# Attention, max-MoE and SoLU-MoE in one kernel: the h blocks of the first two token pairs loaded by two thirds, in other places, with no load held for them

## The chip, the cores and the metric

The kernel runs on one core of one Trainium2 chip. The metric is device microseconds of one execution. Before the change the median of 3 runs is 658.96 us (658.83 to 658.99).

## The reference, cut to what matters

```python
def _attn_ref(q, k, v):                      # 4 batches, 12 heads, 448 tokens, head 64
    scores = matmul(q, k.T) / sqrt(64) - log(448)
    attn = 1 / (1 + exp(-scores))
    return matmul(attn, v)

def _moe_ref(x, w1, w2, w3, w_out):          # x: 1792 tokens x 768
    h = maximum(maximum(x @ w1, x @ w2), x @ w3)
    return h @ w_out

def _moe2_ref(x, w_in, w_out, g_ln):         # w_in: 768 x 1024, w_out: 1024 x 768
    h = x @ w_in
    sm = softmax(h)                          # exp(h - max) / (sum + 1e-9)
    solu = h * sm
    ln = (solu - mean(solu)) / sqrt(var(solu) + 1e-6) * g_ln
    return ln @ w_out

out = _moe2_ref(_moe_ref(_attn_ref(q, k, v), ...), ...)
```

All arrays are float32.

## The kernel before, in words

Every float32 operand of a large product is split in two parts, hi and lo, and the product is three matmuls (hi hi, hi lo, lo hi). A split is a cast on ScalarE (L51) for hi and a subtraction on VectorE (L56) for lo. The large products use a recursion of seven products in place of eight (P1 to P7, table `PROD`): their operands are sums of quarter blocks, named A11, A12, A22, S1 to S4 on one side and B11, B21, B22, T1 to T4 on the other.

The stages:

- Attention for 24 pairs of heads. Beside it `w_out` of the first MoE and `w_in` of the second are multiplied into one matrix, whose seven operands go to DRAM (`w_d`, seven pieces of 128x3x1024 words, 1536 KB each, called B11 to T4 in the list `LOADS`).
- The products of x with w1, w2, w3, in 18 units: nine groups of weights (`gi`) by two batch pairs (`bp`). The last group takes batch pair 1 first, then batch pair 0. `sums` takes the maximum over the three weights in the tiles `hs` and stores every finished third of h (`fp`) to DRAM, `h_d` (L675, L679). The raw words of the weights come through five buffers `raw` (`RAWS`), issued by GpSimd (L141).
- The L stage: h times the fused matrix, in 7 pairs of token tiles. For each pair the four blocks `a` of h are loaded from `h_d` by SP (`load_h`, L710), `prep_l` makes the seven operands from them, and then come P1 (B11), P2 (B21), P6 (T2), P5 (T1), P7 (T3), and behind the next pair's P1 still P4 (T4) and P3 (B22), nine matmuls each. TensorE's timeline names them XL, ZL, XL, VL, XL, XL, VL. The seven weights `wf` are loaded once, by GpSimd (`load_wf`, L739), in the order of `LOADS`.
- Between the two lies `solu_ln`, the normalisation: exponential, squares, a few steps of two columns (`st`), a pair of activations `h`, a transposition on VectorE, a store and a load. Its steps wait in the queue `lazy`.
- The O stage: the second product, again 7 pairs, twelve matmuls a product.

Where the weights of the L stage land is memory that the unit before still uses, so their places come free one after the other: `sa` (tags 0, 1) after the seventh product of the last unit of batch pair 1, `sb` (2, 3, 4) two products later in the next unit, `sc` (5, 6) when the last unit of all is done (L1180 to L1184).

Before the change the first pair's blocks lie in the pool `afirst`. They are loaded by two thirds (the third third of h is not yet in DRAM) and the last third is copied by VectorE out of `hs` (`last_rows`). Between the load of B11 and that of B21 GpSimd makes two small copies of these blocks into a tile `gate` (`hold`, L735), so that B21 is issued only when they have landed:

```python
load_wf(LOADS[0], 0)
load_h(0, 0, slice(0, 2))
load_h(0, 1, slice(0, 2))
for k in range(2):
    hold(hts[(0, 1, k)][:, :8])
last_rows(0)
load_wf(LOADS[1], 1)
```

The order of work on TensorE, ScalarE and VectorE is the order in which the program is written. GpSimd's is pinned from the last units on (`loads`); SP's is set by the scheduler. Work for the next product is interleaved by generators: `run_bg` in the x stage, at a rate per matmul (`RATE`), and `pace(dt)` in the L and O stages: each matmul gives a credit of `dt` microseconds, and steps of `bg`, and then of `lazy`, are taken while credit is left, each with a cost. `product_c` has `dt` 0.227 for the L stage and 0.174 for the O stage.

Of the kernel before, what the change touches and what calls it, by code (L numbers as in the profile page):

```python
# [6 lines left out]
F32 = mybir.dt.float32  # L7
# [8 lines left out]
P = 128  # L16
B, H, S, D = 4, 12, 448, 64
# [11 lines left out]
HU = 384  # L29
QU, OU = 192, 96  # L30
NG = 3 * FC // 2
RAWS = 5
# [12 lines left out]
def sigmoid_attention_max_moe_solu_ln(tc, q, k, v, w123, wo, wi, w2, g, out):  # L45
# [3 lines left out]
    def copy(eng, dst, src):  # L49
        if eng is act:  # L50
            act.copy(dst, src)  # L51
        else:
            eng.tensor_copy(dst, src)
# [68 lines left out]
    raws = {}  # L122
# [199 lines left out]
    def run_bg(n=1):  # L322
        while n > 0 and bg:
            if next(bg[0], "end") == "end":
                bg.popleft()
            else:
                n -= 1
# [324 lines left out]
    def sums(u, i, j, ps, add):  # L652

        gi, bp = u
        fp, w = divmod(gi, 3)
        b = 2 * bp + j
        if (i, b) not in hs:
            nm, n = FIN[len(hs)]
            while (1, nm, n) in fts:
                run_bg()  # L660
            hs[(i, b)] = f_tile(nm, n, f"hs{i}_{b}")
        h = hs[(i, b)]
        if w == 0:
            if add is None:
                act.copy(h, ps)
            else:
                tt(h, ps, add, ALU.add)
        elif add is None:
            tt(h, ps, h, ALU.max)
        else:  # L670
            tt(add, ps, add, ALU.add)
            tt(h, add, h, ALU.max)
        if w == 2:
            to, c = h_d[i, bp][:, :, fp], j * D
            sp.dma_start(  # L675
                out=to[4 * j : 4 * j + 3].rearrange("t p c -> p t c"),
                in_=h[:, c : c + 3 * P].rearrange("p (t c) -> p t c", t=3),
            )
            sp.dma_start(out=to[3, :, c : c + D], in_=h[:, 3 * P * (1 - j) :][:, :D])  # L679
# [16 lines left out]
    hts = {}  # L696

    def h_tile(p, i, k):
        if p % 2:
            t = f_tile(*FIN[4 + i + 2 * k], f"a{p}_{i}{k}")[:, :HU]  # L700
        else:
            t = afirst.tile([P, HU], F32, tag=f"a{i}{k}", name=f"a{p}_{i}{k}")
        hts[(p, i, k)] = t
        return t.rearrange("p (f t) -> p f t", f=3)

    def load_h(p, k, rows=slice(0, 3)):

        for i in range(2):
            bp, t = divmod(tiles[2 * p + i], TT // 2)
            sp.dma_start(out=h_tile(p, i, k)[:, rows], in_=h_d[k, bp][t][:, rows])  # L710

    def last_rows(k):

        for i in range(2):
            t = tiles[i]
            b, c0 = divmod(t * P, S)
            copy(dve, hts[(0, i, k)][:, 2 * P :], hs[(k, b)][:, c0 : c0 + P])

    units = [(gi, bp if gi < NG - 1 else 1 - bp) for gi in range(NG) for bp in range(2)]
    bg.extend(split_t(1, nm, i) for nm, i in FIN)  # L720
# [12 lines left out]
    def hold(view):  # L733

        pool.tensor_copy(gate, view)  # L735

    def load_wf(nm, tag):
        t = wfs[("L", nm)] = wslot[tag].tile([P, 3, 2, 512], F32R, tag=f"s{tag}", name=f"wf{nm}")
        pool.dma_start(out=t.bitcast(F32).rearrange("p c a b -> p c (a b)"), in_=w_d[nm][:, :, : 2 * 512])  # L739
# [125 lines left out]
    for n, u in enumerate(units):  # L865
        if n % 2 == 0:
            late = run_steps(convert_w2(key) for key in w2_left[n // 2])
            lead = 14 if len(w2_left[n // 2]) > 1 else 4
            bg.append(mix(late, convert_group(u[0] + 1), lead) if u[0] + 1 < NG else late)
        tick.update(n=0, done=0, rate=RATE[n // 2])  # L870
        X = ps_x.tile([P, 512], F32, tag="x", name=f"x{n}")[:, :S]
        product(X, u, "P1", True, False)
        e1 = held(u, "e1", X)
        if old is not None:
            product(old["X"], old["u"], "P4", False, True)
            sums(old["u"], 1, 0, old["X"], None)
            product(old["V"], old["u"], "P3", False, True)
            sums(old["u"], 0, 1, old["V"], old["u2"])
            if old["u"] == (NG - 1, 1):
                run_bg(1 << 20)  # L880
                shut(xc_cm, xb_cm)
                wslot.update(weight_slots("sb", (2, 3, 4)))
                hf_cm, hfirst = open_pool("hfirst", 2)
                last_rows(1)
                for k in range(2):
                    load_h(1, k)
                for tag in (2, 3, 4):
                    load_wf(LOADS[tag], tag)
        Z = ps_z.tile([P, 512], F32, tag="z", name=f"z{n}")[:, :S]
        product(Z, u, "P2", True, True)  # L890
        sums(u, 0, 0, Z, e1)
        product(X, u, "P6", False, False)
        u2 = held(u, "u2", X)
        if n == len(units) - 1:
            bg.append(prep_l(0))
        V = ps_v.tile([P, 512], F32, tag="v", name=f"v{n}")[:, :S]
        product(V, u, "P5", True, False)
        product(X, u, "P7", False, False)
        u3 = held(u, "u3", X)
        sums(u, 1, 1, V, u3)  # L900
        if u == (NG - 1, 1):
            loads = pin(ET.Pool)
            shut(xd_cm)
            wslot.update(weight_slots("sa", (0, 1)))
            af_cm, afirst = open_pool("afirst", 1)
            load_wf(LOADS[0], 0)
            load_h(0, 0, slice(0, 2))
            load_h(0, 1, slice(0, 2))
            for k in range(2):
                hold(hts[(0, 1, k)][:, :8])  # L910
            last_rows(0)
            load_wf(LOADS[1], 1)
        old = dict(u=u, X=X, V=V, u2=u2)
    assert not raws and state["load"] == len(stream)

# [24 lines left out]
    def product_c(ps, kind, p, name, start, stop):  # L940
        a, bn = PROD[name]
        key = (kind, p, a)
        while key not in cops:
            assert step(bg), key
        hl = cops.pop(key)
        wt = wfs[(kind, bn)]
        chunks, dt = (3, 0.227) if kind == "L" else (4, 0.174)
        for c in range(chunks):
            for i, (l, m) in enumerate(((0, 0), (0, 1), (1, 0))):
                pe.matmul(  # L950
                    ps,
                    lhsT=hl[l][:, c * P : (c + 1) * P],
                    rhs=wt[:, c, m],
                    start=(start and c == 0 and i == 0),
                    stop=(stop and c == chunks - 1 and i == 2),
                    skip_group_check=True,
                )
                if c == chunks - 1 and i == 2:
                    spent.add(key)
                pace(dt)  # L960
# [208 lines left out]
    for n, (kind, g) in enumerate(groups):  # L1169
        p, last = g[-1], n == len(groups) - 1  # L1170
        if prev and len(prev) > 1:
            for o in prev:
                fourth(o)
        now_open = [begin(kind, g[0])]
        if n == 0:
            product(old["X"], old["u"], "P4", False, True)
            sums(old["u"], 1, 0, old["X"], None)
            product(old["V"], old["u"], "P3", False, True)
            sums(old["u"], 0, 1, old["V"], old["u2"])
            for cm in (xat_cm, xau_cm, xa_cm, st_cm, raw_cm):  # L1180
                shut(cm)
            wslot.update(weight_slots("sc", (5, 6, 7), side="right"))
            for tag in (5, 6):
                load_wf(LOADS[tag], tag)  # L1184
            t_cm, tp = open_pool("tp", 2, side="right")
            act.preload_act_table_set("natural_log_exp_and_others")
        else:
            close(prev)
        now_open += [begin(kind, p) for p in g[1:]]
        if n == 2:  # L1190
            load_w2(LOADS[0], 7)
        if (kind, p) == ("L", NP2 - 1):
            load_u(1)
        if not last:
            for o in now_open:
                second(o)
        if (kind, p) == ("O", 1):
            load_u(2)
        for o in now_open:
            sixth(o)  # L1200
        if kind == "L":
            if p + 2 < NP2:
                next_h(p + 2)
            if p == NP2 - 2:
                load_u(0)
            bg.append(prep_l(p + 1) if p + 1 < NP2 else in_turn(prep_o(0), prep_o(1), 1))
        elif not last:
            bg.append(prep_o(p + 1))
            if 1 < p < NP2 - 2:
                load_u(p + 2)  # L1210
        for o in now_open:
            fifth(o)
        for o in now_open:
            seventh(o)
        if (kind, p) == ("O", 1):
            load_u(3)
        if last:
            for o in now_open:
                second(o)
        prev = now_open  # L1220
# [61 lines left out]
```

## Time and profile before

| | |
|---|---|
| median of 3 runs | 658.96 us |
| profiled execution | 658.38 us |
| its span | 656.6 us |
| TensorE busy | 637.8 us (97%) |
| VectorE busy | 490.7 us (75%) |
| ScalarE busy | 373.4 us (57%) |
| GpSimd busy | 72.6 us (11%) |
| granted clock, mean | 0.992 |

The span runs from the first to the last event on the core; the execution's time is 1.8 us longer. A timeline row gives the start, the length, the engine, the line, what is written from what, how many instructions are merged, and in brackets how long the engine stood idle before, with what ended it. SPq and POOLq are the queues in which SP and GpSimd issue DMAs. A windows row gives busy time by engine in one stretch, then the granted clock of TensorE (PEclk, 1.00 is full speed), the mean busy share of the core's 16 DMA engines, and what they moved. Releasers are inferred: where the engine named had long been done, it was another.

### The profile page before, as it was taken

The page shows a single profiled execution, that of the slowest core. Times are in us where ns is not written, and L with a number is a line of the kernel's source. Part 1 is how long each engine was busy: PE and PEld are TensorE (multiplying, and loading weights), DVE is VectorE, ACT ScalarE, POOL GpSimd, SP SyncE. Part 2 cuts the span into 40 slices and gives each one's busy share as a digit, 9 for nine tenths or more (in the row PEclk, how much of TensorE's full clock was granted, in tenths as well). Part 3 has the DMA queues.
Part 4 walks back from the last instruction along what each step waited for, and adds up shares of the span by engine and source line. Part 5 has one row for each costly group of instructions (what it writes and reads, how often), then busy time and mean ns, then how long its engine had stood idle before and what let it go on. Part 6 is the DMA issues. An engine that isn't in the chain of part 4 may idle for free.

```text
span 656.6 us, 9719 instructions
## 1 busy us (share of the span) xinstructions
PE 637.8 (97%) x3283; PEld 519.3 (79%) x3283; DVE 490.7 (75%) x1070; ACT 373.4 (57%) x712; POOL 72.6 (11%) x147
## 2 busy tenths in 40 slices
PE   9999999999999999999999999977999999999897
PEld 6555588754557999999999999955877889999897
DVE  4799987599547788886888678544688879687672
ACT  5888523578866545455455454222666674766551
POOL 2111121000100101101101100112000035300000
PEclk9999999999999999999999999997999999999999
DMA  8688668853710346765468543899336269956151
GB/s 292 216 256 260 220 199 303 314 211 109 259 33 0 105 125 188 215 166 163 131 176 233 168 121 90 248 374 407 130 108 182 58 205 385 311 180 185 59 168 70
DMA packets 85921, 125.17 MB, mean 191 GB/s; under 512 B 39024, under 2 KB 65648, under 8 KB 85872
## 3 DMA queue, kind: packets, MB, share of 16 engines
q1 hardware_dynamic: 74288, 70.84, 34.2%
q0 software_dynamic: 11440, 53.48, 25.2%
q8 instruction: 26, 0.43, 0.3%
q10 hardware_dynamic: 144, 0.23, 0.1%
q14 instruction: 23, 0.19, 0.1%
HBM read 84.15 MB, written 40.37 MB: 190 GB/s over the span
## 4 chain that ended last, share of the span: by engine, by line
PE 65%; DVE 16%; ACT 6%; DMA 6%; issue 5%; SPq 1%; POOL 0%; DVEq 0%; ACTq 0%; POOLq 0%
PE x L644 19%; PE v L644 9%; PE XO L950 7%; PE av L272 6%; PE z L644 5%; PE XL L950 5%; PE sc L251 4%; PE VO L950 4%; PE VL L950 2%; PE ZO L950 2%; DMA wfT<-w_dT 2%; ACT e L998 2%; PE sc L247 1%; DMA wfB<-w_dB 1%; ACT h L1014 1%
## 5 line engine op out<-in xcount | busy, mean ns | idle before, releaser
L272 PE MATMUL av<-sf,vr 128*64 128x448 f32 x384 | 77.5, 545 | 0.0
L259 ACT ACTIVATE sf<-sc,bias_s 128x896 f32<-128x896 f32 x72 | 67.9, 1013 | 2.4
L141 POOL DMA_DIRECT2D raw<-in_w x52 | 28.0, 539 | 277.3 <-DVE S L56 138.4
L272 PEld LDWEIGHTS av<-sf,vr 128*64 128x64 f32 x384 | 25.4, 136 | 40.9 <-issue 34.4
L251 PE MATMUL sc<-qt,kt 64*128 64x448 f32 x432 | 51.1, 375 | 1.5 <-ACT sf L256 1.5
L473 PE MATMUL pw<-wi_t,r_wo 128*128 128x512 f32 x216 | 49.6, 390 | 0.0
L251 PEld LDWEIGHTS sc<-qt,kt 64*128 64x128 f32 x432 | 39.0, 184 | 11.7 <-issue 4.3
L473 PEld LDWEIGHTS pw<-wi_t,r_wo 128*128 128x128 f32 x216 | 40.4, 188 | 9.4 <-issue 1.0
L689 ACT COPY u<-x 128x448 f32<-128x448 f32 x36 | 19.1, 530 | 44.3 <-PE x L644 44.3
L950 PE MATMUL XL<-wfT,c_L_S 128*128 128x512 f32 x126 | 33.1, 409 | 4.1 <-DMA wfT<-w_dT 3.1
L644 PE MATMUL x<-T3h,S 128*128 128x448 f32 x108 | 33.7, 366 | 0.0
L644 PE MATMUL x<-B11h,A 128*128 128x448 f32 x108 | 33.7, 366 | 0.0
L644 PE MATMUL x<-T4h,A 128*128 128x448 f32 x108 | 33.6, 365 | 0.0
L644 PE MATMUL x<-T2h,S 128*128 128x448 f32 x108 | 33.6, 365 | 0.0
L644 PE MATMUL v<-B22h,S 128*128 128x448 f32 x108 | 33.6, 365 | 0.0
L644 PE MATMUL z<-B21h,A 128*128 128x448 f32 x108 | 33.6, 365 | 0.0
L644 PE MATMUL v<-T1h,S 128*128 128x448 f32 x108 | 33.6, 365 | 0.0
L950 PEld LDWEIGHTS XL<-wfT,c_L_S 128*128 128x128 f32 x126 | 24.3, 196 | 11.3 <-issue 4.2
L413 ACT ACTIVATE raw<-raw,g_sb 128x192 f32<-128x192 f32 x32 | 13.3, 466 | 31.3 <-DVE raw L157 31.3
L950 PE MATMUL XO<-w2tT,c_O_S 128*128 128x384 f32 x168 | 31.1, 336 | 0.0
L157 DVE SCALAR_TENSOR_TENSOR raw<-raw 128x384 int32<-128x384 int32 x52 | 29.0, 557 | 1.1
L950 PEld LDWEIGHTS XO<-w2tT,c_O_S 128*128 128x128 f32 x168 | 29.3, 188 | 0.0
(185 smaller groups left out, 1547.1 us busy)
## 6 DMA issues: line engine op xcount, KB each, us to landing
raw<-in_w POOLq DMA_DIRECT2D x52, 384.0 KB, 4.1
w_d<-w2s SPq DMA_DIRECT2D x48, 192.0 KB, 2.4
u_d<-h SPq DMA_DIRECT2D x56, 128.0 KB, 2.9
ut<-u_d SPq DMA_DIRECT2D x14, 512.0 KB, 5.3
kr<-in_k SPq DMA_DIRECT2D x24, 256.0 KB, 3.5
vr<-in_v SPq DMA_DIRECT2D x24, 256.0 KB, 3.9
raw<-in_wi POOLq DMA_DIRECT2D x16, 384.0 KB, 4.9
w_dT<-wsT SPq DMA_DIRECT2D x12, 512.0 KB, 3.7
```

What stands on the lines that cost most here:

```text
L141: pool.dma_start(out=t, in_=source(key).rearrange("p (n t) -> p n t", t=2))
L157: dve.scalar_tensor_tensor(out=yi, in0=raws[key][:, cols, 0], scalar=29, in1=yi, op0=ALU.logical_shift_right, op1=ALU.bitwise_or)
L247: pe.matmul(sc[:, 0, :S], lhsT=kt[:, x, c * P :], rhs=qt[:, y], start=start, stop=stop)
L251: pe.matmul(sc[:, j, :S], lhsT=kt[rows, x, c * P : (c + 1) * P], rhs=qt[rows, y], start=start, stop=stop)
L259: act.activation(sf, sc[:, :, :S], AF.Sigmoid, bias=bias_s, scale=1.0 / math.sqrt(D))
L272: pe.matmul(pa[j * D : (j + 1) * D, :S], lhsT=vr[:, j, c], rhs=sf if c == 3 else sf[:, j], start=(n == 0), stop=(n == 3),)
L413: act.activation(half, half, AF.Copy, scale=g_sb[:, kc + 4 * i : kc + 4 * i + 1])
L473: pe.matmul(ps, lhsT=wt[:, a, cols], rhs=wi_t[:, b, c0 : c0 + 512], start=(i == 0), stop=(i == 3 * KC - 1))
L644: pe.matmul(ps, lhsT=l, rhs=r, start=(start and c == 0 and i == 0), stop=(stop and c == 2 and i == 2), skip_group_check=True)
L689: act.copy(e, ps)
L950: pe.matmul(ps, lhsT=hl[l][:, c * P : (c + 1) * P], rhs=wt[:, c, m], start=(start and c == 0 and i == 0), stop=(stop and c == chunks - 1 a ...
L998: act.activation(e[i], h[i], AF.Square, bias=su[:, c], scale=-float(F2), accum_out=vs[:, c])
```

## The change

The tiles of the first pair's blocks move to two of the five `raw` buffers, the second pair's to `afirst`, and the later pairs change places with each other. The first pair's loads are written two products earlier, in the last unit of batch pair 1. The second pair too is loaded by two thirds, and `last_rows` copies its last third for both halves. The two `hold` copies go, so that B11 and B21 stand next to each other on GpSimd. The first pair must be prepared before the pool of `raw` is closed. And the credit of a matmul in the O stage is 0.19 for 0.174.

```diff
     def h_tile(p, i, k):
-        if p % 2:
+        if p == 0:
+            if i == 0:
+                state["a", k] = rawp.tile([P, 2, HU], F32, tag="raw", name=f"a0_{k}", bufs=RAWS)
+            t = state["a", k][:, i]
+        elif p % 2 == 0:
             t = f_tile(*FIN[4 + i + 2 * k], f"a{p}_{i}{k}")[:, :HU]
         else:
             t = afirst.tile([P, HU], F32, tag=f"a{i}{k}", name=f"a{p}_{i}{k}")
...
-    def last_rows(k):
+    def last_rows(p, k):
 
         for i in range(2):
-            t = tiles[i]
-            b, c0 = divmod(t * P, S)
-            copy(dve, hts[(0, i, k)][:, 2 * P :], hs[(k, b)][:, c0 : c0 + P])
+            to, at = 2 * P, tiles[2 * p + i] * P
+            while to < HU:
+                b, c0 = divmod(at, S)
+                n = min(HU - to, S - c0)
+                copy(dve, hts[(p, i, k)][:, to : to + n], hs[(k, b)][:, c0 : c0 + n])
+                to, at = to + n, at + n
...
                 hf_cm, hfirst = open_pool("hfirst", 2)
-                last_rows(1)
+                last_rows(0, 1)
                 for k in range(2):
-                    load_h(1, k)
+                    last_rows(1, k)
                 for tag in (2, 3, 4):
                     load_wf(LOADS[tag], tag)
...
         sums(u, 0, 0, Z, e1)
+        if u == (NG - 1, 1):
+            while state["load"] < len(stream) or len(raws) > RAWS - 2:
+                run_bg()
+            for k in range(2):
+                load_h(0, k, slice(0, 2))
         product(X, u, "P6", False, False)
...
             af_cm, afirst = open_pool("afirst", 1)
-            load_wf(LOADS[0], 0)
-            load_h(0, 0, slice(0, 2))
-            load_h(0, 1, slice(0, 2))
             for k in range(2):
-                hold(hts[(0, 1, k)][:, :8])
-            last_rows(0)
-            load_wf(LOADS[1], 1)
+                load_h(1, k, slice(0, 2))
+            for tag in (0, 1):
+                load_wf(LOADS[tag], tag)
+            last_rows(0, 0)
...
-        chunks, dt = (3, 0.227) if kind == "L" else (4, 0.174)
+        chunks, dt = (3, 0.227) if kind == "L" else (4, 0.19)
...
             sums(old["u"], 0, 1, old["V"], old["u2"])
+            while ("L", 0) not in prepared:
+                assert step(bg)
             for cm in (xat_cm, xau_cm, xa_cm, st_cm, raw_cm):
                 shut(cm)
```

Three places of the instruction order. On SP's queue in the last unit of batch pair 1 (`w2_d` is a store of a staged piece of w2, `a0_` a load of the first pair's h):

```order
 L433 DMA w2_d2_108<-w2s3_1_2_4211 512x1x96
 L433 DMA w2_d3_109<-w2s3_1_3_4227 256x1x96
+L714 DMA a0_0_4393<-h_d01_111 128x256 x2
+L714 DMA a0_1_4396<-h_d11_113 128x256 x2
 L433 DMA w2_d0_106<-w2s3_2_0_4348 512x1x96
 L433 DMA w2_d1_107<-w2s3_2_1_4358 512x1x96
```

The first pair's four loads come ahead of eight stores of w2 and four of h that they stood behind; in their old place stand four loads of the second pair, of the same shape.

On ScalarE in the first group of the O stage, before (`u20`, `u21` are copies out of the products P6 of pairs 0 and 1, `c_O_1_S3` is the hi part of pair 1's S3, L998 to L1014 are steps of the normalisation):

```order
L1142 COPY u20_5559<-XO0_5562 128x384
L998 ACTIVATE e1_5488,st4_5176<-h1_5125,st4_5176 128x1024
L998 ACTIVATE e2_5490,st4_5176<-h2_5126,st4_5176 128x1024
L1000 ACTIVATE st4_5176<-st4_5176,eps_z_186 128x2
L1003 ACTIVATE st4_5176<-st4_5176 128x2
L1004 ACTIVATE st4_5176<-st4_5176 128x2
L51 CAST c_O_0_A22_5724<-ut8_5340 128x512
L1142 COPY u21_5617<-XO1_5620 128x384
L51 CAST c_O_1_S3_5734<-ut10_5451 128x512
L1014 ACTIVATE h1_5125<-h1_5125,st4_5176 128x1024
L1014 ACTIVATE h2_5126<-h2_5126,st4_5176 128x1024
```

And of the changed kernel, the same place:

```order
L1152 COPY u20_5561<-XO0_5564 128x384
L1008 ACTIVATE e1_5490,st4_5178<-h1_5127,st4_5178 128x1024
L1008 ACTIVATE e2_5492,st4_5178<-h2_5128,st4_5178 128x1024
L1010 ACTIVATE st4_5178<-st4_5178,eps_z_186 128x2
L1013 ACTIVATE st4_5178<-st4_5178 128x2
L1014 ACTIVATE st4_5178<-st4_5178 128x2
L1024 ACTIVATE h1_5127<-h1_5127,st4_5178 128x1024
L1024 ACTIVATE h2_5128<-h2_5128,st4_5178 128x1024
L1152 COPY u21_5619<-XO1_5622 128x384
L51 CAST c_O_0_A22_5746<-ut8_5342 128x512
L51 CAST c_O_1_S3_5753<-ut10_5453 128x512
```

The two activations `h` have moved ahead of the copy `u21` and of two casts.

On ScalarE at pair 4 of the O stage, before (`u24` and `u34` are copies out of pair 4's P6 and P7):

```order
L1142 COPY u24_6177<-XO4_6180 128x384
L51 CAST c_O_5_A11_6277<-ut3_6131 128x512
L998 ACTIVATE e5_6149,st6_5453<-h5_5376,st6_5453 128x1024
L998 ACTIVATE e6_6151,st6_5453<-h6_5377,st6_5453 128x1024
L1000 ACTIVATE st6_5453<-st6_5453,eps_z_186 128x2
L1003 ACTIVATE st6_5453<-st6_5453 128x2
L1004 ACTIVATE st6_5453<-st6_5453 128x2
L1014 ACTIVATE h5_5376<-h5_5376,st6_5453 128x1024
L1014 ACTIVATE h6_5377<-h6_5377,st6_5453 128x1024
L1153 COPY u34_6178<-XO4_6180 128x384
```

And of the changed kernel:

```order
L1024 ACTIVATE h6_5379<-h6_5379,st6_5455 128x1024
L51 CAST c_O_4_S1_6235<-os1_4_6138 128x512
L1102 COPY cx3_6040<-XO3_6041 128x384
L51 CAST c_O_4_S3_6266<-ut2_5992 128x512
L51 CAST c_O_4_A22_6273<-ut2_5992 128x512
L51 CAST c_O_4_S4_6280<-ut1_5990 128x512
L1152 COPY u24_6193<-XO4_6196 128x384
L51 CAST c_O_5_A11_6308<-ut3_6139 128x512
L51 CAST c_O_5_A12_6323<-ut3_6139 128x512
L1163 COPY u34_6194<-XO4_6196 128x384
```

The last chain of the normalisation has moved from between `u24` and `u34` to the pair before. TensorE's order is the same in both kernels, and ScalarE's and VectorE's up to the O stage too, but for the added copies.

## Rows read from the trace of the kernel before

**Rows 1.** Waits of TensorE in the O stage: total, times, longest, us

```profile
PE XO L950 <- ACT u L1153: 1.7, 1, 1.7
```

**Rows 2.** Timeline of TensorE, 425 to 540 us: start, length, instruction, [idle before]

```profile
435.01 2.35 PE L950 MATMUL ZL<-wfB,c_L_A 128*128 128x512 f32 x9 [1.92 <-DMA wfB<-w_dB]
440.12 3.09 PE L950 MATMUL XL<-wfT,c_L_S 128*128 128x512 f32 x9 [2.77 <-DMA wfT<-w_dT]
445.57 4.21 PE L950 MATMUL VL<-wfT,c_L_S 128*128 128x512 f32 x9 [2.35 <-DMA wfT<-w_dT]
...
459.21 2.32 PE L950 MATMUL VL<-wfB,c_L_S 128*128 128x512 f32 x9 [1.89 <-DMA wfB<-w_dB]
461.36 2.22 PE L950 MATMUL ZL<-wfB,c_L_A 128*128 128x512 f32 x9
463.43 2.22 PE L950 MATMUL XL<-wfT,c_L_S 128*128 128x512 f32 x9
```

**Rows 3.** Windows: busy by engine, PEclk, DMA share, GB/s

```profile
400.00:405.00 5.00, 5.00 (x27) 4.63 (x26) 3.14 (x7) 1.97 (x5) 0.13 (x1) 1.00 0.24 79
...
415.00:420.00 5.00, 5.00 (x26) 4.63 (x26) 2.32 (x6) 0.87 (x3) 0.75 (x1) 1.00 0.91 254
...
425.00:430.00 5.00, 5.00 (x25) 4.40 (x24) 4.61 (x10) 3.01 (x8) 2.12 (x3) 1.00 0.91 268
...
445.00:450.00 5.00, 4.21 (x9) 2.81 (x9) 3.38 (x7) 1.34 (x3) 0.77 (x1) 0.50 1.06 401
```

**Rows 4.** Timeline of GpSimd, 400 to 660 us

```profile
415.08 0.75 POOL L739 DMA_DIRECT2D wfB<-w_dB  x1 [14.95 <-PE x L644]
424.47 0.19 POOL L735 COPY gate<-a 128x8 f32<-128x8 f32 x1 [8.63 <-DMA a<-h_d]
...
425.90 0.79 POOL L739 DMA_DIRECT2D wfB<-w_dB  x1
426.69 0.76 POOL L739 DMA_DIRECT2D wfT<-w_dT  x1
435.27 0.77 POOL L739 DMA_DIRECT2D wfT<-w_dT  x1 [7.83 <-issue]
```

**Rows 5.** DMA issues, 415 to 425 us: count, KB each, us to landing

```profile
wfB<-w_dB POOLq DMA_DIRECT2D x1, 1536.0 KB, 8.1
```

**Rows 6.** Timeline of SP's queue, 395 to 440 us

```profile
406.57 3.46 SPq L433 DMA_DIRECT2D w_d<-w2s  x4
...
417.50 2.37 SPq L710 DMA_DIRECT2D a<-h_d  x4
```

**Rows 7.** DMA queues, 425 to 435 us: packets, MB, share of 16 engines

```profile
q1 hardware_dynamic: 1835, 1.32, 43.8%
```

**Rows 8.** DMA queues, 440 to 450 us (q0 GpSimd's, q1 SP's)

```profile
q0 software_dynamic: 830, 3.27, 79.7%
q1 hardware_dynamic: 1323, 0.79, 25.1%
```

**Rows 9.** Instructions on the tiles a: duration ns min/median/max, first and last start

```profile
L53 DVE COPY a<-hs x4: 220/220/221, 416.4 to 421.4; 128x128 f32<-128x128 f32 x4
```

**Rows 10.** Timeline of VectorE, 420 to 485 us

```profile
424.72 0.56 DVE L56 TENSOR_TENSOR c_L_A<-a,c_L_A 128x384 fp32r<-128x384 f32 x1 [1.45 <-ACT c_L_A L51]
```

**Rows 11.** Timeline of ScalarE, 540 to 657 us

```profile
559.30 1.15 ACT L998 ACTIVATE e<-h,st 128x1024 f32<-128x1024 f32 x1
...
614.38 1.15 ACT L998 ACTIVATE e<-h,st 128x1024 f32<-128x1024 f32 x1
...
618.63 2.37 ACT L1014 ACTIVATE h<-h,st 128x1024 f32<-128x1024 f32 x2 [1.02 <-DVE st L1010]
620.91 0.46 ACT L1153 COPY u<-XO 128x384 f32<-128x384 f32 x1
621.27 0.62 ACT L51 CAST c_O_A<-ut 128x512 fp32r<-128x512 f32 x1
```

**Rows 12.** Timeline of TensorE, 539 to 657 us

```profile
564.97 4.33 PE L950 MATMUL XO<-w2tT,c_O_S 128*128 128x384 f32 x24
```

## Prediction

> **What bounds the kernel now.** I first read TensorE's list of waits by stage: in the O stage it holds one wait, 1.7 us [rows 1]; the others that matter are for the weights `wf` of the L stage, between 433 and 460 us. Then the TensorE timeline of that stretch [rows 2]. The old work ends at 435.01 - 1.92 = 433.09. From there seven products of the first L pair run until ZL of the second pair starts at 461.36: 28.3 us. At the undisturbed pitch of 463.43 - 461.36 = 2.07 us they would take 14.5. So 13.8 us are lost here, part as waits (1.92 for B21, 2.77 for T2, 2.35 for T1, 1.89 for B22), part as slow products: VL took 4.21 us where it takes 2.2 to 2.3 elsewhere, at a granted clock of 0.50, the lower level of 1.2 GHz [rows 2, 3]. This is the stage to price.
>
> Why are the weights late? The reader is to see in the GpSimd timeline [rows 4] that B11 is issued at 415.08, that GpSimd then stands for 8.63 us until the loads of h land (the two copies into `gate`), and that B21 goes only at 425.90. T2 follows at once; T1 goes at 435.27, when B21 has landed (ZL starts at 435.01), so two weights are in the queue at a time and the third waits for the first. But the DMA engines do not stand still meanwhile: their share is 0.91 from 415 to 420 and again from 425 to 430, and 1.06 later [rows 3].
>
> **The change part by part.** *The hold goes.* B21 is issued right behind B11, at 415.08 + 0.75, some 10 us earlier. B11 itself landed 8.1 us after issue, at 423.2 [rows 5], with the same h traffic beside it, and I leave that. What the engines gain is only the time in which they stood: 0.09 x 5 us twice, 0.9 us [rows 3].
>
> *Bytes leave the stretch.* SP issues the four loads of the first pair's h (128x256 words, 128 KB each) at 417.50; in the changed order they stand ahead of the stores of the last two pieces of w2 and wait only for buffers whose words the last weight group has used up; the first of those stores is issued at 406.57 [rows 6]. From 400 to 405 the DMA share is 0.24 [rows 3], so there they cost nothing. The second pair loads 128x256 where it loaded 128x384, four times 64 KB less, and moves up to the first pair's place in the queue. Together 0.52 + 0.26 = 0.79 MB. SP's queue moved 1.32 MB in 43.8% of 10 us, 301 GB/s [rows 7], so that is 2.6 us of engine time.
>
> *When the last weight lands.* It lands now at 459.1 (VL starts at 459.21). Late bound: all else keeps its place, and it gains 0.9 + 2.6 = 3.5 us: 455.6. Early bound: from 423.2 the GpSimd queue always has two weights in it and runs as from 440 to 450, when it had 79.7% of the engines and moved 3.27 MB in 10 us beside SP's 25.1% [rows 8]; six weights of 1.57 MB (1536 KB) are 9.44 MB, 28.9 us: 452.1. SP's traffic would then be put off, which hurts nobody soon: the second pair's h is needed only some 10 us later. Neither end is nearer to a row of its own, so I take the middle, 453.9, a pitch of 5.1 us: B21 428.3, T2 433.4, T1 438.6, T3 443.7, T4 448.8, B22 453.9.
>
> *What TensorE then waits for.* Its order is unchanged. ZL at 433.1 and XL with T2 at 435.2 find their weights; the product with T1 starts at 438.6 instead of 437.2, that with T3 at 443.7, the second pair's first one at 445.8, T4 at 448.8, B22 at 453.9. About 8 us of waiting are left where 13.8 were lost, and VL ends at 456.0: **5.4 us earlier** than 461.36 (bounds 3.7 and 7.2). From there the L stage is the same program, shifted.
>
> *The copies.* Six more VectorE copies of 128 or 64 columns, at most 0.22 us each, 1.3 us, behind those at 421 [rows 9]. VectorE next stands 1.45 us before 424.72, waiting for ScalarE [rows 10]; that hides them. Without it the first split of the L stage would come 1.3 us later, and its product with it. The places of raw words cost nothing: their old contents are converted before; that the first pair must be prepared before T4's and B22's places are taken is no wait, since TensorE itself frees them only at 433.1.
>
> *The pace of the O stage, 0.174 to 0.19.* The pieces of the normalisation come earlier among the evictions. Today's one stall, 1.70 us, is `u34`, an eviction of pair 4, which stands behind the chain from the squares at 614.38 to the pair of activations `h`, which ends at 621.00 [rows 1, 11]. In the new order that chain begins a pair earlier and nothing of it stands ahead of pair 4's `u34`; the 1.70 goes. What may be late next: in the first O group the same chain now runs before `u21` and the cast of S3. It takes 621.00 - 614.38 = 6.6 us undisturbed; from 559.30 it ends at 565.9, then 0.46 for the eviction and two casts of 0.62, 567.6, while the product that reads S3 starts at 564.97 + half of 4.33 = 567.1 [rows 11, 12]. So up to 0.5 us for the first half of the split, more for its second half on VectorE and for the next pair's A11, which now stands behind two long VectorE steps. I take 1.2 us as an estimate, between nothing and one more stall of 1.70 in each of two places (3.4). The O stage nets a gain of 0.5 (from +1.7 to -1.7).
>
> *The sum.* 5.4 + 0.5 = 5.9 us. The profiled execution took 658.38 us (span 656.6, 1.8 around it), 0.58 below the median of 658.96; from 658.38 it is 652.5, and on the median **653.1**. Its own range, from the bounds: 650 to 657.
>
> **The rivals.** *The engines are the bound and the clock takes its part* (18%). If SP's traffic is served as before, B22 lands at 455.6, and with the waits left TensorE may stand at the lower clock again, as from 445 to 450 [rows 3]; VL then takes 4.2 us and ends at 459.8. Gain 1.6 + 0.5: 656.9; without the clock 654.8. For it: 13.8 us of loss stand beside engines that are full. Against it: in the early part of the stretch GpSimd's queue had only B11 and left SP alone for three microseconds, and that order does change. The Trainium skill, DMA: Bandwidth & Descriptors, section Issuing engines are not separate DMA queues, says that all issuers end on the same 16 engines and interleave. By that rule an earlier issue adds no bandwidth, and only the bytes and the idle time count, 3.5 us; the trace agrees in the share of 1.06.
>
> *The hold was the whole delay* (17%). Every weight moves up by the 9.8 us of B21's issue: B22 at 449.3, VL done at 451.4, gain 10.0 + 0.5: 648.5. For it: the chain of issue and landing that starts with B21. Against it: in those 9.8 us SP's queue moved bytes that must go somewhere.
>
> *The change does nothing* (6%). SP's stores and loads take the time that the hold gave them anyway, the last weight still lands at 459, and the O stage is even: 658.5 to 659.
>
> *Slower, by the pace of the O stage* (7%). Seven evictions or casts in ScalarE's new order stand behind squares, exponentials or the pair `h`. If each costs the 1.70 of today's one, that is 11.9, less 1.7 and 5.4: 4.8 us slower, 663.8. It decides from five such stalls on (8.5 against 7.1). Against it: each product's eviction has another product of 2.1 us between it and its reader, and by the sum above most find 1 us to spare.
>
> **How the numbers follow.** Forecast 52%, the others as named. Leaving out most of the slow case, the empty one and a little of the fastest, 648.5 to 656.9 holds 8 in 10. No change is within 0.2%, 1.3 us, about what a measurement of this kernel can tell: 6%, the empty case; slower 7%; faster 87%.
>
> **What would show it.** In the changed profile: no copy into `gate` before 460, and B21 issued within 1 us of B11; B21 landed before 433, so that ZL starts without a wait; then waits for T1, T3 and B22, 1 to 3 us each; B22's product starting between 452 and 456, and ZL of the second pair between 454 and 458; the DMA share at 1.0 until then, and some 0.3 or more between 400 and 405. In the O stage the wait of 1.70 gone, and a smaller one at the first group. The forecast is wrong if the last weight lands later than 456 or earlier than 452, if TensorE's clock is low when B22's product runs, if ZL of the first pair starts later than 433.1, or if the O stage shows more than two waits over 1 us.

## The result, and the profile after

The changed kernel takes 653.84 us (median of 4 runs, 652.22 to 654.87); the kernel before, on the same chip, 658.98 (658.83 to 659.12). The ratio is 0.9911 [0.9891, 0.9931]: faster by 5.1 us. The profiled execution is the shortest of the four: 652.22 us, span 650.1, mean granted clock 1.000. The other three took 653.76, 653.92 and 654.87 us at a mean clock of 0.995.

TensorE's timeline after, the stretch of [rows 2]:

```profile
433.20 2.23 PE L960 MATMUL ZL<-wfB,c_L_A 128*128 128x512 f32 x9
435.27 2.23 PE L960 MATMUL XL<-wfT,c_L_S 128*128 128x512 f32 x9
438.79 2.35 PE L960 MATMUL VL<-wfT,c_L_S 128*128 128x512 f32 x9 [1.29 <-DMA wfT<-w_dT]
443.62 2.30 PE L960 MATMUL XL<-wfT,c_L_S 128*128 128x512 f32 x9 [2.48 <-DMA wfT<-w_dT]
...
448.73 2.29 PE L960 MATMUL XL<-wfT,c_L_A 128*128 128x512 f32 x9 [0.74 <-ACT h L1132]
453.67 2.29 PE L960 MATMUL VL<-wfB,c_L_S 128*128 128x512 f32 x9 [2.65 <-DMA wfB<-w_dB]
455.80 2.24 PE L960 MATMUL ZL<-wfB,c_L_A 128*128 128x512 f32 x9
```

ZL of the first pair no longer waits. The waits left are for T1, T3, T4 and B22, 7.2 us together, and ZL of the second pair starts at 455.80 instead of 461.36: 5.56 us earlier. (The row for T4 names ScalarE; what came in there just before is the weight, issued at 439.05 and landed 9.6 us later.) From this start to the end of the span it is 650.1 - 455.80 = 194.3 us, before 656.6 - 461.36 = 195.2. The 6.5 us between the two spans are 5.56 from the stretch of the weights and 0.94 from behind it. In the times of these two executions 6.16 of it shows (658.38 - 652.22): the time is 2.1 us longer than the span after, and was 1.8 before.

GpSimd's timeline, for [rows 4]:

```profile
415.38 1.53 POOL L746 DMA_DIRECT2D wfB<-w_dB  x2 [14.96 <-PE x L644]
...
434.80 0.76 POOL L746 DMA_DIRECT2D wfT<-w_dT  x1 [6.22 <-DMA h_d<-hs]
439.05 0.77 POOL L746 DMA_DIRECT2D wfT<-w_dT  x1 [3.48 <-DMA h_d<-hs]
443.80 0.76 POOL L746 DMA_DIRECT2D wfB<-w_dB  x1 [3.98 <-issue]
```

B11 and B21 go together, and no copy into `gate` stands between. From T4 on each weight goes out when the second one ahead of it has landed: T4 at 439.05, just behind the start of T1's product (438.79), and B22 at 443.80, just behind that of T3's (443.62).

SP's queue, for [rows 6], and the windows, for [rows 3] (busy by engine, granted clock, DMA share, GB/s):

```profile
400.44 2.28 SPq L714 DMA_DIRECT2D a<-h_d  x4
...
417.80 2.60 SPq L714 DMA_DIRECT2D a<-h_d  x4
```

```profile
400.00:405.00 5.00, 5.00 (x26) 4.64 (x25) 3.43 (x7) 1.77 (x4) 0.42 (x1) 1.00 0.61 188
...
425.00:430.00 5.00, 5.00 (x26) 4.41 (x25) 4.58 (x9) 2.79 (x7) 0.77 (x1) 1.00 1.05 400
...
445.00:450.00 5.00, 4.26 (x20) 3.19 (x19) 2.11 (x5) 2.00 (x4) 1.19 (x3) 1.00 1.04 394
```

The first pair's loads moved 17 us ahead, into engines that had stood at 0.24; from 425 to 430 these now move 400 GB/s where they moved 268. The clock of 0.50 in 445 to 450 is gone in this execution.

The two DMA queues from 425 to 435, for [rows 7] (packets, MB, share of 16 engines; q0 is GpSimd's, q1 SP's):

```profile
q0 software_dynamic: 822, 3.24, 79.1%
q1 hardware_dynamic: 1285, 0.79, 24.9%
```

SP's queue moves 0.79 MB here instead of 1.32, and GpSimd's runs already at the rate that it reached only from 440 on before [rows 8].

The waits of TensorE in the O stage, for [rows 1], and VectorE's first split of the L stage, for [rows 10]:

```profile
PE XO L960 <- DVE c_O_A L56: 0.2, 1, 0.2
PE XO L960 <- DVE c_O_S L56: 0.2, 1, 0.2
PE XO L960 <- ACT c_O_S L51: 0.2, 1, 0.2
```

```profile
425.02 0.56 DVE L56 TENSOR_TENSOR c_L_A<-a,c_L_A 128x384 fp32r<-128x384 f32 x1 [1.20 <-ACT c_L_A L51]
```

The stall of 1.7 us has become three of 0.2. The six new copies did fill a part of VectorE's wait for ScalarE (1.20 for 1.45); the split itself comes 0.30 us later, as B11 does (415.38 for 415.08), and nothing is pushed.

### The profile page after: what moved, and what is told of

Read it like the earlier page. It is cut to its first block, busy times and chain, and to the rows that moved or that the text cites. A ratio compares the mean times of both kernels' runs of the same rounds, so it can differ in the third digit from the quotient of the medians.

```text
span 650.1 us, 9741 instructions
## 1 busy us (share of the span) xinstructions
PE 634.3 (98%) x3283; PEld 517.3 (80%) x3283; DVE 490.4 (75%) x1076; ACT 373.1 (57%) x712; POOL 71.6 (11%) x145
## 4 chain that ended last, share of the span: by engine, by line
PE 66%; DVE 16%; DMA 7%; ACT 5%; issue 5%; SPq 0%; POOL 0%; DVEq 0%; ACTq 0%
PE x L644 19%; PE v L644 9%; PE XO L960 7%; PE av L272 6%; PE z L644 5%; PE XL L960 4%; PE sc L251 4%; PE VO L960 4%; DMA h_d<-hs 3%; PE VL L960 2%; PE ZO L960 2%; PE sc L247 2%; DMA wfB<-w_dB 1%; ACT e L1008 1%; ACT h L1024 1%
## 5 line engine op out<-in xcount | busy, mean ns | idle before, releaser
L689 ACT COPY u<-x 128x448 f32<-128x448 f32 x36 | 19.1, 530 | 44.3 <-PE x L644 44.3
L960 PE MATMUL XL<-wfT,c_L_S 128*128 128x512 f32 x126 | 31.4, 394 | 3.5 <-DMA wfT<-w_dT 2.5
```

Of the source, the lines that this page charges most:

```text
L689: act.copy(e, ps)
L960: pe.matmul(ps, lhsT=hl[l][:, c * P : (c + 1) * P], rhs=wt[:, c, m], start=(start and c == 0 and i == 0), stop=(stop and c == chunks - 1 a ...
```

## The experiments

In each, the kernel before ran on the same chip; ratios are to it. Where two kernels differ in when B11 goes out, I count from the issue of B11 to the start of the product with B22: 44.13 us before (459.21 - 415.08), 38.29 after (453.67 - 415.38). Two profiled executions of one program differ in this count by 0.5 us (the changed kernel has 37.79 in the second profile of experiment 1), two of the old L stage by 0.9 (45.02 in experiment 7).

**1. The waits filled with products.** To take the clock out of the comparisons, 29 matmuls on B11 into a PSUM bank of their own stand in the four waits:

```diff
+    def fill(n):
+        wt = wfs[("L", "B11")]
+        F = ps_f.tile([P, 512], F32, tag="f", name=f"fill{n}")
+        for _ in range(n):
+            pe.matmul(F, lhsT=wt[:, 0, 0, :P], rhs=wt[:, 0, 0], start=True, stop=True)
...
     def fifth(o):
+        if (o["kind"], o["p"]) == ("L", 0):
+            fill(5)
```

and `fill(10)`, `fill(3)` and `fill(11)` ahead of the first pair's P7, P4 and P3.

> The changed kernel with 29 matmuls of no use on TensorE, in one PSUM bank of their own, ahead of the products that wait for weights: 5 before T1's, 10 before T3's, 3 before T4's, 11 before B22's, each about 0.22 us, so that they fit into the waits of 1.3, 2.5, 0.7 and 2.6 us. If the spread of the changed kernel (652.22 at a mean clock of 1.000, 653.76 to 654.87 at 0.995) is TensorE's clock falling in these waits: every execution at a mean clock of 1.000, all times within 652.0 to 652.8. Rival (the spread comes from the DMA): the median stays near 653.8 with the same spread. Rival (fillers get in the way): slower than 654.

Measured: 652.02 us (651.66 to 652.35, 5 runs, clock 0.999 to 1.000), ratio 0.9877 [0.9854, 0.99]. TensorE's timeline:

```profile
450.67 2.70 PE L977 MATMUL fill<-wfB 128*128 128x512 f32 x11
453.40 2.32 PE L961 MATMUL VL<-wfB,c_L_S 128*128 128x512 f32 x9
```

The weights land where they landed (38.08 us from B11's issue to the product with B22). To see the two side by side I ran both again on one chip.

> The changed kernel as it is, beside the one with fillers on the same chip. Theory that its own spread is TensorE's clock in the waits for weights: between 652 and 655 us, the executions at a mean granted clock of 1.000 near 652.2, those at 0.995 near 654; median 653 to 654.5. Rival, that the spread is the chip's and not the clock's: the same spread with and without fillers.

> The changed kernel with 29 filler products in the waits, beside the changed kernel on the same chip. Theory that the clock alone makes the spread: all executions at 0.999 to 1.000 and within 1 us of 652.0, so the median 1 to 2.5 us below the kernel without fillers. Rival, that the spread is the chip's: the medians within 0.5 us of each other.

Measured: the changed kernel 653.31 us (651.75 to 655.65, 6 runs), ratio 0.9906 [0.9887, 0.9926]; with fillers 652.06 (651.57 to 652.56, 5 runs), ratio 0.9887 [0.987, 0.9903]. The spread shrinks from 3.9 to 1.0 us and the median by 1.25; the intervals of the two ratios still overlap. So most of the spread is what TensorE does in the waits. It isn't the mean clock alone: the profiled execution of the changed kernel had 0.996 and took 651.75, the shortest of its six. Its timeline and one window:

```profile
443.42 3.87 PE L960 MATMUL XL<-wfT,c_L_S 128*128 128x512 f32 x9 [2.46 <-DMA wfT<-w_dT]
...
453.16 2.30 PE L960 MATMUL VL<-wfB,c_L_S 128*128 128x512 f32 x9 [1.71 <-DMA wfB<-w_dB]
```

```profile
440.00:445.00 5.00, 2.54 (x9) 1.76 (x8) 2.67 (x6) 1.34 (x3) 1.35 (x2) 0.84 0.99 352
```

T3's product took 3.87 us, partly at the lower level of the clock, and the wait for B22 behind it shrank from 2.65 to 1.71: a slow product ahead of a wait costs nothing. One behind the last wait must cost; no execution of 654 us was profiled, so which product is slow there stays open.

**2. The hold put back.** On the kernel with fillers, the two copies into `gate` return, now for the second pair's blocks, which stand where the first pair's stood:

```diff
-            for tag in (0, 1):
-                load_wf(LOADS[tag], tag)
+            load_wf(LOADS[0], 0)
+            for k in range(2):
+                hold(hts[(1, 1, k)][:, :8])
+            load_wf(LOADS[1], 1)
```

> after_fill with the two gate copies back between B11 and B21, now on the second pair's blocks (the first pair's are loaded long before). If the wait in GpSimd's queue is what made the weights late: B21 issued near 426, ZL of the first pair waits for it 1 to 3 us, B22's product starts between 456 and 457 (459.2 less the bytes moved away, 2.6), time near 655.0. Rival (the moved bytes were the gain): B22 at 453.5 as in after_fill, time 652.0.

Measured: 657.3 us (656.72 to 660.06, 12 runs), ratio 0.9956 [0.9939, 0.9974]; the kernel before 659.63 there. That is 2.3 us more than expected: the hold costs more than that text allowed for. GpSimd's timeline, TensorE's product with B22, and the load of B22 (KB, us from issue to landing); the profiled execution, 660.02 us, runs some 3.3 us later from before B11 on:

```profile
418.65 0.75 POOL L747 DMA_DIRECT2D wfB<-w_dB  x1 [15.35 <-PE x L645]
428.11 0.19 POOL L743 COPY gate<-a 128x8 f32<-128x8 f32 x1 [8.71 <-DMA a<-h_d]
...
429.55 0.79 POOL L747 DMA_DIRECT2D wfB<-w_dB  x1 [0.18 <-issue]
...
451.90 0.76 POOL L747 DMA_DIRECT2D wfB<-w_dB  x1 [3.55 <-issue]
```

```profile
461.84 2.21 PE L963 MATMUL VL<-wfB,c_L_S 128*128 128x512 f32 x9
```

```profile
wfB<-w_dB POOLq DMA_DIRECT2D x1, 1536.0 KB, 9.4
```

The product starts 43.19 us after B11's issue, against 38.08 without the hold. But the eleven fillers ahead of it keep it back here: B22 itself landed at 451.90 + 9.4 = 461.3, 42.65 us after B11's issue. Without the hold it landed 37.9 after (443.83 + 9.4 - 415.32), in the kernel before 44.0 (450.25 + 8.8 - 415.08). So the hold alone costs 4.7 us (5.3 in the medians of the times), and the moved bytes bring 1.3 while it stands, 2.2 if the other execution of the old L stage is taken. That the hold is the larger part is clear; the size of the smaller part is not.

Where the 4.7 us go is seen first in SP's queue from 427 to 430 (GpSimd's moved nothing there) and in the window behind it:

```profile
q1 hardware_dynamic: 1759, 0.92, 100.1%
```

```profile
430.00:432.00 2.00, 2.00 (x11) 1.72 (x10) 1.93 (x4) 1.11 (x3) 1.10 (x2) 1.00 0.44 50
```

Then it is seen in what SP's queue moved from B11's issue to B22's landing: with the hold,

```profile
q1 hardware_dynamic: 6743, 3.89, 31.0%
```

without it (experiment 1),

```profile
q1 hardware_dynamic: 5053, 2.86, 24.7%
```

and in the kernel before:

```profile
q1 hardware_dynamic: 7307, 4.66, 34.1%
```

While GpSimd stands and B11 has landed, the engines don't stand: SP's stores and loads, which no product needs yet, fill them. Only behind the late issue of B21 do they fall to 0.44 for 2 us. Up to the last landing SP's queue moves 1.03 MB more with the hold, 13.2 us of all engines for 9.4 (31.0% of 42.65 and 24.7% of 37.95): 3.8 of the 4.7 us. The rest is about the time in which the engines stand. The kernel before moves 0.77 MB more again, which are the bytes that the change takes out of the stretch.

**3. The hold taken away, alone.** The kernel before, less the two `hold` lines and nothing else.

> The kernel before, without the two gate copies; h loads, tiles and pace as before. If the weights' issue decides: B21 issued within 1 us of B11, the weights land at a pitch of about 5 us from 423, VL of the first pair (B22) starts near 454 instead of 459.2, time near 654.5. The price should be seen at the start: the first pair's h then lands some 10 us after issue at 417.5, about 428, and the first XL of the L stage starts 3 to 5 us later than 427.2, which is hidden as the later weights are waited for anyway. Rival (the moved and saved h bytes are the gain, the hold is nothing): B22 at 458 or later, time 658 to 659. Second rival (the late start of the first XL shifts all): time above 658.

Measured: 656.53 us (653.38 to 659.27, 10 runs), ratio 0.9946 [0.992, 0.9971]: 2.7 us below the kernel before on that chip, about half of the gain, and 2.0 more than expected. The spread is wide: the shortest execution is within the changed kernel's range, and the profiled one is the longest of the ten, so it shows the price at its worst; none of the short ones was profiled. The first pair's loads (KB, us to landing), then ScalarE's, TensorE's and GpSimd's timelines:

```profile
a<-h_d SPq DMA_DIRECT2D x4, 128.0 KB, 11.2
```

```profile
428.61 0.51 ACT L51 CAST c_L_A<-a 128x384 fp32r<-128x384 f32 x1 [3.44 <-DMA a<-h_d]
431.49 0.51 ACT L51 CAST c_L_A<-a 128x384 fp32r<-128x384 f32 x1 [2.37 <-DMA a<-h_d]
```

```profile
436.82 0.74 PE L644 MATMUL x<-T4h,A 128*128 128x448 f32 x1 [5.17 <-ACT u L689]
...
442.31 2.24 PE L948 MATMUL ZL<-wfB,c_L_A 128*128 128x512 f32 x9
```

```profile
442.88 0.77 POOL L739 DMA_DIRECT2D wfT<-w_dT  x1 [8.31 <-DMA h_d<-hs]
```

Now B21 fills the engines beside the first pair's h, whose loads take 11.2 us to land where they took 6.1 with the hold; the casts wait, the copy `u` stands behind them on ScalarE, TensorE waits 5.17 us for it in the old stage, and with that stage the places of T4 and B22 come free late: T4 goes out at 442.88, where it goes at 439.05 in the changed kernel. So the price that was expected at the start came, and in this execution it was not hidden. The hold had protected these loads. It can go because the first pair no longer loads at that place: in the changed kernel those engines carry the second pair's blocks, whose first cast comes at 438.02 instead of 424.48.

**4. Bytes added.** On the kernel with fillers, four more stores of 128 KB (0.52 MB, about what the first pair's loads were) ahead of the second pair's loads (cut: `extra` is a list of four DRAM tiles):

```diff
+            for n in range(4):
+                sp.dma_start(out=extra[n], in_=hs[(1, 3)][:, : 2 * P])
```

> after_fill with four more stores of 128x256 words on SP's queue, into DRAM that nothing reads, just ahead of the second pair's loads: the 0.52 MB that the change moved out of the stretch are put back into it. If the DMA engines' total work sets when the last weight lands: B22's product starts 1.7 us later, near 455.1, time 653.7. Rival (GpSimd's queue takes its 79 per cent whatever SP has waiting, SP's traffic is only put off): B22 moves by less than 0.5, time 652.0 to 652.5, and SP's own loads and stores land later.

Measured: 653.91 us (653.75 to 656.65, 6 runs), ratio 0.9922 [0.9904, 0.9941]. B22's product comes 455.56 - 415.83 = 39.73 us after B11's issue: 1.65 later, as by total work. TensorE's timeline, and what SP's queue moved from B11's issue to B22's landing (2.86 MB without the added stores):

```profile
455.56 2.29 PE L964 MATMUL VL<-wfB,c_L_S 128*128 128x512 f32 x9 [0.43 <-DMA wfB<-w_dB]
```

```profile
q1 hardware_dynamic: 5507, 3.36, 27.1%
```

**5. Bytes removed.** On the kernel with fillers, the stores of h's last third for the tokens of the blocks that are copied (0.52 MB, read by nobody) are left out; fillers 4, 8, 3 and 9.

```diff
+            copied = u == (NG - 1, 1)
+            if copied and j == 0:
+                return
             sp.dma_start(
...
+            if copied:
+                return
```

> after_fill without the stores to DRAM that nothing reads any more: of the last third of h for batch pair 1, the parts of the token tiles of the first two pairs, which VectorE now copies (two stores of 192 KB, four of 32 KB, 0.52 MB), and with 4, 8, 3 and 9 fillers. If the total work of the DMA engines sets the last weight's landing: B22's product starts 1.7 us earlier or more, the stores being of small pieces, near 451.5, time 650.2. Rival (SP's traffic is only put off): 652.0.

Measured: 651.87 us (651.4 to 654.29, 5 runs), ratio 0.9885 [0.9867, 0.9903]. B22's product comes 453.71 - 416.03 = 37.68 us after B11's issue, 0.4 earlier and not 1.7, and 0.4 is no more than two executions of one program differ by. SP's queue over the same stretch, with the stores left out:

```profile
q1 hardware_dynamic: 5106, 2.97, 25.5%
```

It moves no less than the 2.86 MB of experiment 1. SP's later transfers move up into the room, here the third pair's loads (three of them go out at 438.60 instead of 440.65). Bytes put ahead of the weights delay them; bytes taken away are replaced by the next in SP's queue.

**6. SP's queue held instead.** If SP's share sets the pitch, holding SP should give the weights the engines. A tiny store that reads T3 (then, in the second kernel, T1) stands in SP's queue ahead of all that follows; the stores of experiment 5 are left out too. The edit, cut to its main lines:

```diff
+                quiet = pin(ET.SP)
+                sp.dma_start(out=mark, in_=wfs[("L", "T3")][:, 0, 0, :8].bitcast(F32))
+                for k in range(2):
+                    load_h(2, k)
```

> The changed kernel with fillers (0, 2, 3 and 10) and without the stores of h that nothing reads, and with SyncE's queue held: a tiny store of a piece of weight T3 stands in it, so the loads of the third pair's h blocks and every later transfer of that queue wait until T3 has landed. Theory that SyncE's backlog sets the weights' pitch (it took 20 to 28% of the engines' time from 425 to 455 us): alone on the engines the weights come some 0.9 us closer together, T3 at about 439.6, T4 at 444.5, the product with the last weight at 449 to 451 us instead of 453.4, so 33.5 to 35.5 us after B11's issue instead of 37.7; the kernel takes 648 to 650 us. Rival, that GpSimd's own queue sets the pitch: the last weight stays at 37 to 38 us after B11's issue, 652 us. Second rival: the third pair's h then comes too late for its casts and the later products wait for it, 650 to 653 us with the wait at the casts of a<-h_d.

> The same with SyncE's queue held only until weight T1 has landed (fillers 1, 6, 3 and 10). Theory that SyncE's backlog sets the weights' pitch: T1 comes some 2 us earlier, the weights behind it at the old pitch, so the product with the last weight 35 to 36.5 us after B11's issue and 649.5 to 651 us. Rival, GpSimd's own queue sets the pitch: 37 to 38 us after B11's issue, 652 us.

Measured: held for T3 652.27 us (651.53 to 652.67, 4 runs), ratio 0.9897 [0.9883, 0.9912]; held for T1 651.39 (650.88 to 652.38, 4 runs), ratio 0.989 [0.9874, 0.9907]. The theory falls: B22's product comes 38.83 and 37.48 us after B11's issue, not 35. The queues from 435 to 445, held for T3 and then in experiment 1, and TensorE's timeline of the first:

```profile
q0 software_dynamic: 849, 3.35, 92.2%
q1 hardware_dynamic: 73, 0.03, 1.2%
```

```profile
q0 software_dynamic: 796, 3.13, 83.5%
q1 hardware_dynamic: 1011, 0.56, 19.1%
```

```profile
438.97 2.34 PE L971 MATMUL VL<-wfT,c_L_S 128*128 128x512 f32 x9 [1.39 <-DMA wfT<-w_dT]
...
442.72 2.31 PE L971 MATMUL XL<-wfT,c_L_S 128*128 128x512 f32 x9 [0.94 <-ACT c_L_S L51]
...
448.98 2.32 PE L971 MATMUL XL<-wfT,c_L_A 128*128 128x512 f32 x9 [1.21 <-issue]
...
454.27 2.31 PE L971 MATMUL VL<-wfB,c_L_S 128*128 128x512 f32 x9 [0.66 <-DMA wfB<-w_dB]
```

Alone on the engines, GpSimd's queue moves 3.35 MB in 10 us where it moved 3.13 beside SP's 0.56: it does not fill them by itself. T3 follows T1 by 3.75 us instead of 4.83, and then T4 takes 6.26, though SP's queue has no more than 9.5% from 443 to 449 (0.17 MB): why T4 comes so late there stays open. What was gained is given back.

**7. The pace of the O stage, both ways.** In the kernel before `dt` 0.174 becomes 0.19, in the changed one 0.19 becomes 0.174, nothing else.

> The kernel before with 0.19 for 0.174 as the O stage's credit per matmul, nothing else. If the O stage's part of the gain is the pace: from ZL of the second L pair to the end 194.3 us instead of 195.2, the wait of 1.7 us at pair 4 gone and three waits of about 0.2 in the first groups, time 658.0. Rival (the O stage gained because the L stage came earlier): unchanged, 658.9.

> The changed kernel with 0.174. If the pace is worth 0.9 us by itself: the wait of 1.7 us is back and the time is 0.9 above the changed kernel's, near 654.8 on the median and 653.1 in an execution whose clock stays at full. Rival: no difference.

Measured: before with 0.19 657.97 us (657.51 to 660.03, 12 runs), ratio 0.9976 [0.9961, 0.9992]; after with 0.174 653.49 (652.07 to 654.96, 6 runs), ratio 0.9899 [0.9875, 0.9924], which with the clock's spread can't be told from 653.84. The traces separate them. Before with 0.19 (ZL of the second pair; its span is 656.7, so 194.3 us to the end) has the three waits of 0.2, after with 0.174 has the old one:

```profile
462.36 2.24 PE L950 MATMUL ZL<-wfB,c_L_A 128*128 128x512 f32 x9
```

```profile
PE XO L960 <- ACT u L1163: 1.7, 1, 1.7
...
455.55 2.22 PE L960 MATMUL ZL<-wfB,c_L_A 128*128 128x512 f32 x9
```

With 0.174 it is 650.8 - 455.55 = 195.25 us to the end: the pace is worth 0.9 us of the span, with or without the rest. Between the two profiles of the changed kernel only 0.35 of it shows in the time (652.57 and 652.22), which is 1.8 us longer than the span with 0.174 and 2.1 with 0.19.

## Why the prediction was right, and which terms were off

**What bounds the kernel.** Right: the loss by late weights was the place. Of 13.8 us between 433 and ZL of the second pair 8.1 are left (455.80 - 433.20 - 14.5); the prediction said about 8.

**When the last weight lands.** Right in its result, and in part by luck: the products with T1, T3, T4 and B22 were put at 438.6, 443.7, 448.8 and 453.9 and started at 438.79, 443.62, 448.73 and 453.67. But the middle between two bounds was a choice without a row of its own, and the terms of the late bound were mis-sized against each other. *The hold* was priced at the time in which the engines stood, 0.9 us; put back by itself it costs 4.7 (experiment 2). The idle time is about that; the 3.8 us of SP's bytes that pass the weights meanwhile were not in the sum. *The bytes* were priced at 2.6 us; with the hold in place they brought 1.3 to 2.2, adding two thirds of as many costs 1.65, taking that many more away brings at most 0.4 (experiments 4, 5; one profile each). Full engines did not mean that the right bytes moved: from 427 to 430 of experiment 2 they moved SP's alone. The early bound had the mechanism (SP's traffic is put off, and nobody needs it soon), and it missed by 1.6 us as GpSimd's queue does not keep its share for six weights: from 440 to 450 it has 72.0% and moves 2.77 MB, where the bound took 79.7% and 3.27 throughout:

```profile
q0 software_dynamic: 708, 2.77, 72.0%
```

The Trainium skill, DMA: Bandwidth & Descriptors, section Queues, rings and completion order, says that each DMA engine takes turns between the queues that have work for it, a packet at a time. The trace agrees in kind: with a weight always in the queue, GpSimd's packets get 79.1% from 425 to 435 beside SP's 24.9; with B11 landed and B21 held, SP's get 100.1% (427 to 430 of experiment 2). An earlier issue adds nothing to the engines' busy share where that is full, as the first rival held, but it buys a share in the turns.

**The hold was the whole delay** (17%). The cause was this rival's; its size was not. B22 moved by 5.5 us and not by the 9.8 of B21's issue: until 423.2, 7.1 us of the 9.8, B11 was still on its way and used the engines, and SP's queue still takes its quarter.

**The engines are the bound and the clock takes its part** (18%). The first half fell: B22's product came at 453.67, not 455.6. The second half was missing from the forecast: three of four executions are 1.5 to 2.7 us longer than the profiled one, and with the waits filled the median falls to 652.0. The sum on the profiled execution gave 652.5 and it took 652.22; the median of 653.1 was passed by 0.7 by this. The prediction thus rests its closeness on the median partly on small errors that work against each other: 0.4 too little from the O stage, 0.3 by which the time now exceeds the span by more than before, and no price for the clock.

**Copies and places.** Right: VectorE's first split comes when it came, and nothing waits for it.

**The pace of the O stage.** Right in kind: 1.70 goes and a smaller stall comes in the first O group, at the two halves of the split of S3 and at the next A11. Sized at 1.2 us, these are 0.16, 0.19 and 0.24, and the net gain is 0.94 instead of 0.5. Of the seven stalls by which the slower rival came out, none shows above 0.25 us.

**Signs named in advance.** They held in the profiled execution: B21 right behind B11, ZL without a wait, four waits under 3 us, B22's product between 452 and 456, the DMA share at 1.0 to 1.06 from 420 on (0.91 from 415 to 420) and 0.61 from 400 to 405, no low clock when B22's product runs. One limit was drawn too tight: ZL of the first pair was not to start later than 433.1 and starts at 433.20, without a wait, in an execution whose B11 goes out 0.30 later than before.

**Still open.** Some executions of several kernels, at full clock, are 2 to 3 us longer (656.4 and 656.65 in experiment 4, 654.29 in 5). None of these was profiled, but the profile of experiment 2 is one of three long executions of its kernel (660.02), and it shows where its 3 us lie. From 260 to 412 us, where its program is that of experiment 1, TensorE has no idle time and a granted clock of 1.00 in both profiles, and yet it runs 738 matmuls where the other runs 752. What slows them, and whether the others are of this kind, stays open.

## What to carry to other kernels

When DMA engines are full, ask whose bytes they move: a load that is held back loses its share to whatever else is queued, and the idle time of the engines is only a part of a hold's price (0.9 of 4.7 us here). Where a hold protects a transfer, that transfer has to move too: without the hold alone the times spread over 5.9 us and the median gained 2.7, with the whole change 5.1. And where TensorE waits several times in a row, filling the waits with products that nobody reads makes the times of a comparison steady (3.9 to 1.0 us here), and is itself worth 1.25 us of the median.

## What was not expected of the hardware

Adding and removing bytes on SP's queue are not mirror images: 0.52 MB more delayed the last weight by 1.65 us, 0.52 MB less brought 0.4 (one profile each), no more than two executions of one program differ by. GpSimd's queue alone, with two weights of 1.57 MB in it at most, did not fill the 16 engines in experiment 6: 92.2% by itself against 83.5% and 19.1% together. TensorE's matmuls can come 2% further apart over 150 us with no wait and no lower granted clock (738 for 752, experiment 2). And a product of 3.87 us at the lower clock level, where the next wait is longer than what it lost, left the execution at 651.75, the shortest of six.
